# The first batch of an attention and feed-forward kernel worked in two parts of its tokens

## The chip, the cores and the metric

The kernel runs on one core of a Trainium2 chip. The core has five engines that work at the same time: TensorE (PE) multiplies matrices, VectorE (DVE) and ScalarE (ACT) work element by element and can read the accumulators (PSUM), GpSimd (POOL) does the same without access to PSUM, and SyncE (SP) only issues transfers (DMA). The metric is the device time of one execution in microseconds (us), lower is better, given as the median of several runs.

## What is computed

For 8 batches, 8 heads, 576 tokens and a head width of 64, attention with a threshold, then a feed-forward layer with a maximum over three products:

```python
scores = scale * np.matmul(q, k.transpose(0, 1, 3, 2))
thresh = np.max(scores, axis=-1, keepdims=True) - tau
scores = np.where(scores >= thresh, scores, -1000000000.0)
attn = softmax(scores)
x = (attn @ v).transpose(0, 2, 1, 3).reshape(4608, 512)
h = np.maximum(np.maximum(x @ w1, x @ w2), x @ w3)   # 512 -> 768
out = h @ w_out                                       # 768 -> 512
```

## The kernel before

**Units of work.** Four heads of one batch make a quad, so there are 16 quads, two for each batch. The 576 query tokens of a quad's heads are worked in nine chunks of 128 rows, and each chunk in two halves `r` of 576 columns (one head, or two half heads). Chunk `c` below 4 and chunk `c + 5` hold the same token block of 128 for the two pairs of heads; chunk 4 holds the last 64 tokens of both. So the softmax of the whole kernel is 144 chunks, 288 halves.

**One half.** PE makes its scores in one of four PSUM slots (`scores`, L285; letter `S`). DVE takes their maximum and writes a copy `z` (`maximum`, L327; `m`). ACT makes a first exponential or a leaky clamp (`exponents`, L342; `e`), and then either ACT makes the exponential with its sum (`n`) or DVE multiplies by the mask with its sum (`k`) (`numerators`, L352). The digits of `MASKED` (L24) choose the form for each half: 1 and 3 leave the mask to DVE, 2 and 3 let ACT read the scores from PSUM instead of `z` (`direct`, L312), and digit 0 needs one more small DVE instruction for the threshold (`s`). When both halves of a chunk are summed, DVE makes the reciprocals (`r`), POOL writes the normalized `P` in bf16 (`p`, two instructions, L366), and SP issues a DMA that transposes `P` into `ptq` (`t`, L376). There are nine buffers for `z`, six for `P`, two for `ptq`, and four PSUM slots for everything that PE writes.

**Around it.** Loads of q, k and v (`l`); transposes of q and k on PE (`T`) with their copies to `qt` (ACT, `a`) and `kt` (mostly DVE, `c`); a copy of `qt` with its halves swapped (`q`, POOL, for the first quad partly DVE); casts of v (`y`, POOL); loads of the 12 weight pieces of 512 KB (`g`, SP) into two staging buffers and their casts (`z`, POOL). The staging buffers serve as two more `z` buffers after half 72.

**Products and feed-forward.** When a quad's chunks are transposed, PE multiplies them with v (`product`, L381; `O`), and DVE and ACT copy the result to `xt` (`w`, `x`). When both quads of a batch are there, the feed-forward of the batch (`ffn`, L440) makes 18 pieces `hid` (six blocks of 128 hidden columns, three weights each; `F`, and `B` for the second half of a whole piece). The first of three is copied by ACT (`h`, tile `hm`), the other two are folded in by DVE with a maximum (`v`, tiles `hm` and `hT`). Then follow two output pieces of two token blocks each (also `F` and `B`, copied out by ACT, `u`, stored by SP, `o`) and one for the last 64 tokens (`N`, `j`, `i`).

**The split.** `SPLIT` (L38) names batches that are worked in two parts of their tokens: blocks 0 and 1 (256 tokens), then blocks 2, 3 and 4 (320 tokens). For such a batch `steps` (L553) lists the chunks of the first part for both quads, then those of the second part for both quads; `products` (L591) and `ffn` make products and 18 hidden pieces for each part. A piece of a part uses all 128 rows of PE at once and has 4 matmuls of 256 or 320 columns; a piece of a whole batch has 16 matmuls of 64 rows and 288 columns, of which two run side by side. Before the change only batch 7, the last, is split.

**The order.** Everything is issued in the order of the string `ORDER` (L40), one letter for each step as named above; a digit behind `S`, `T`, `O`, `F` or `N` is the PSUM slot. Each engine keeps this order (`_Ordered`, L84), so an engine that waits holds up all that stands behind it on that engine. The loop that reads the string is at the end of the kernel:

```python
while x < len(text):
    what = text[x]
    if what in "STOFN":
        x += 1
    issue(what, int(text[x]) if what in "STOFN" else None)
    x += 1
```

Since every instruction passes through one helper, the profile names line 93 for nearly all of them, and groups are told apart by their tiles.

Of the kernel before, what the change touches and what calls it, by code (L numbers as in the profile page):

```python
# [39 lines left out]
ORDER = """  # L40
llllllllT0T1gacgT2qqlaT1lqqS2clS1lmlS0zmlS3mlS2enemlznmS1lS3ersmlpS2eklS0pelmnlmyS3germeS1plkptS2eemnT0mlmS1
lrS3enskplelermlpnT2smS1tnpS3mapmtT0qascqeT0rS2tpecmepS0nkqtS1nT2rmnqmlepslkeS3ylakeS2rmynplS0epgmeS1tpsmeyT
3rnmS2tnpS1npmnystrS2rmpespemS0eqctT2mqT3enkpS0lnssS1rlaplnS2lqermtpemS0pesS1clpnmlS3npmlertmpnkS1petresT2mn
pS0keqlS3rtempmpkS0tpS1mennasrtremS2pempmS3ytzeseS2mS0pnmS1npmS2nytssmT0erceT1pleO3pmlektO0swernpgS3nlpmalwk
S3nlrS1xmlpnS0mlpeS3tmyT1eS2rssmpnS0spemeymO2zeceygO0wntrkpS3xwrS2nsstS0pmnF1pmnBtpsesF2mF3hqrT0nyBqaF1rsveB
zF0vnT2qgT3clqBaBzhS3evF1qgnmtBpS0evpS3nrF2mlpS1eslmpS0ntmyS3pesmS1pnslmS0ztBrmT3hpF1ceF2pgeBmlzF3esvlBnBgvF
1etkF0hBrkepBtsnvS3S2nprmeS1ptmF3epvBrqmtS0hS2spmeS3zsmS1leF0lsknpF2nBmBeytmS3essvS1qerlkO0pngerslvpnlmO2pnm
pnrswS3peS1wremzF0emBqgnktpS1hS3xmS0nptmS2pF1rsmepBtsnF0vT3sraS1mteBqT2evT3pnmS0ptacS1zemS3eS2pmeS0ztmemqnF3
mlerklpeS2sBlkelpeF1mlklS2klS0leuunrsmS3pnoBkpnlmelO2uqmlnrlkO3ptwrqrT2weexkS0uptF3nmS1BsysclF0phmF2tyeBpseS
1vyBetmS3npF0vnS1prmBnptS2mhyS3rspsmS1eS0ytmepF2mnF3pBmelBvlF0enssS1klF2erlmBpeoBvphF1osnF3vlBeklBntS2svT0hr  # L50
rT1mpnF3tcapS2espS0metT1prmBnyF2srvnT0tByceS3qsvaS0plemF1qlnS2mBnqmS0hpS3srsmeF2ptmS1epS0meBptmS3qS1vF0penns
smF2yteBmBersvS1phT3sskpF0aT2keF3mnBrBqtnvO1pnveprN0rceptS3wnpS2mjS1ptsS0mepS3rmeF2ptmnpmnS0BsetkekS3urlmpS1
ulmeqS0lmT2epS3mlaS1nmlO2nrlmplesO3kqoekleO1klewslswxS0pxlrwT2nmS3plS1nrcplF0ermptempS2S3pmlS1penmBoemqonkF3
tF1ekeBkF2lhBrkutpF3uvBBryssvelS1lhS0ympT2lS3matpS1mnS2pseF0ssmtF3emT1eBsrcpF2teBrvpeBpeS0vtS1npmS3nmS0thmF1
nS2smtnF3kF0esBsrmepBsvBnpS2hvtS1nrF0rmpnT3BmlpaS2vlepS1mtS3eqS0mnpF2semF1lBersmopT3nBstcyF0pevO3erktphkBnsF
1weoS2rpvnlF3qmBelBnvqtT2T0hrqsS1capS3lemF2pnS0mptS1nssmBpeS3mytF0evS1nyBmelO2ssrvepmepN3wxktS1nS2rmpnS0mpS1
esrjmyS2tnpS3meF0psrmleptskeT1pS2eBmelmqalS3kqnS2lmS1ntrmeO3puqmuO2oysnswlerkyT0lS3ewlrcF1pxiskepS0emS2tnpmB
nqmelpkS0ulF2puT3lmeBlF1rrskhplS0akF2teBmBnsvpF0tnS3spveBpmS1lhS2srtmepS0meF3pF1esmtyF2ekBnBvtBnsrS0sphrS3mn
lpS2melpF0mntF3pBveqS2ssveBorS1nsmopF0emtpS2eBrvpS1hsmlF3pnS0monT2mlBnF1rclpeF0vlBpeBtvynT3S2shqS1amtF0eykT3
eO2sscterkO3pnmewqBxT1nwqvS2npF3mS0aytsrBrnpmF1espvS2eS0rpmtS3empBS2mphtF0nsspsT3mBeqcF2tnS1veS3rmT0peBmpaS1  # L60
ssvS3eqtS0semqN2nmqlS1mjlnS3klS0nF2lremppmO1yenrtsmeO3wynpipT0xwBcnlrkeplS3kulS0umS1lnS2mpteS3mF0ermpetF1epm
T2BsslkekalF3uklBuF2strrkhpBesBvnS1lpF0voepS3metS2prBmpS1hmtS3pnmF0ynS2rssmptBnS1mpeF3svqetF2sBmeBkeF1lkF0nB
vhBerrvF3pnS2spvBnmptS1eS0rpmhT2epmlT3S1acplF0eosS3mnBtmF1nvT2eF3ktBBssceS0rvhS2pesrO1mpemytnsS3wnpS2mS1lnpm
F0nqtF3ssmeBqBsrevqF1leS2pvlnS0mplBemS3lhF2srmtepS0S1epmF3nmBtnBsrkpT1nvO0npvT2xtwrrS3spacS0eymS1peS2mptS3em
S0pemF1qetmnsskT2BalkelrmS3nlpS2slumqS0elsmpO3eomuoN2erkplO0ekljwelS1rpeoF3kxqtnwS2mnS0ympS1nlF2pmlBqmoenssi
seBkF1khT0iuBrrscpuS2veF0ptS3mnpS1mepS2oemBoF3mF1treesvBpBrkhpT0lF2katS3vnBmnF0ytT1vnBpcS3hpS2tmeS0reF1smpS3
etsmqF2nBmqeT0kF3paBvnBrnstsS1vpS0hrmpeS2mptF1erS3spmeS0spmnlBF2lmqeF3lqsessvBtyeBpvS1hS0rkpntF3mnF2mBpnlS1r
snvpT0tBecpO3metveS0snrwF2plnS1mpS3ermBytepmS0hT1mS3aT2smnT0qN1capnF3rkqF2teBsssesBvqjS0leS1qveS3pmF2nprmnpm
tS0nS1spmnT3ByretrcempS0usS3pumS1eptmS2eF0pmemnS1kBesskermO2pnknyO1keteskyO3xrwuwpuS2wxptS0empS3erS1mptS2emp
F0mF3lBmBlenkhF2ntvS0nS1ssrmBpelF3vpeF0smBteBsrhkF1peF2vBnyS0nvS3pnmO1ntmS0wrsrS3rpesmS1eymBpS0shptmF3nF2pmn  # L70
BprtBevS0peS1vpF3oemF2pnomBoBrhsskpS1teF3veF0mpBetkBS1vhF2tnrkF0pnBmF3esprBveBytvpO2nkO1pxhS0rwS2mptS1mpS0mS
# [649 lines left out]
```

## Time and profile before

| | |
|---|---|
| median of 3 runs | 455.76 us (454.06 to 458.42) |
| the profiled execution | 457.37 us, of which the span from the first to the last instruction is 455.6 us |
| PE, weight loads of PE | busy 429.6 us (94%), 318.8 us (70%) |
| DVE, ACT, POOL | busy 398.0 (87%), 403.5 (89%), 314.7 us (69%) |
| granted clock of PE | 0.984 of full speed as a mean |
| DMA | 87.46 MB, mean 192 GB/s |

The time of a run holds some 1.8 us beside the span. A line of a stage shows the stretch in us from the span's start, its length, then for each engine the busy time and in brackets the number of instructions, and at the end the granted clock of PE, the mean busy share of the 16 DMA engines and what they moved in GB/s. A line of the chain of waits shows start, length and the work that the end of the kernel hung on. A line of a group shows line, engine, operation, written tile and read tiles, their shapes and the count; then busy time in us and the mean of one in ns; then the idle time of the engine just before, and what ended it.

### The profile page before, as it was taken

The numbers are of one execution on the slowest core, as the hardware profiler recorded it, in microseconds if no ns is written. First come the engines' busy times: TensorE is split into PE (matmuls) and PEld (weight loads), VectorE is DVE, ScalarE is ACT, GpSimd is POOL, SyncE is SP. The second block draws the span as 40 slices with busy tenths as digits, with TensorE's granted clock in tenths as the row PEclk, the third lists the DMA queues.
The fourth block names the chain that finished last, engine by engine and source line by source line (L and its number), as shares of the span: only waits on it lengthen the run. The fifth ranks groups of instructions, "written<-read, shape, count | busy, mean of one in ns | idle before, by whom it ended". The sixth has DMA issues, their size and how long they took to land. (4 is left out here: it accounts for less than half of the span.)

```text
span 455.6 us, 14387 instructions
## 1 busy us (share of the span) xinstructions
PE 429.6 (94%) x5188; PEld 318.8 (70%) x5188; DVE 398.0 (87%) x1256; ACT 403.5 (89%) x830; POOL 314.7 (69%) x416
## 2 busy tenths in 40 slices
...
GB/s 261 237 232 177 239 185 201 221 227 266 187 223 179 217 185 231 195 211 197 166 232 201 206 190 226 159 237 159 158 221 198 225 149 124 116 199 127 128 82 105
DMA packets 213287, 87.46 MB, mean 192 GB/s; under 512 B 186336, under 2 KB 200160, under 8 KB 213216
## 3 DMA queue, kind: packets, MB, share of 16 engines
...
## 5 line engine op out<-in xcount | busy, mean ns | idle before, releaser
L93 POOL TENSOR_SCALAR P<-z,rs 128x576 bf16<-128x576 f32 x250 | 202.0, 820 | 77.9 <-DVE rs L93 31.1
L93 DVE TENSOR_SCALAR_CACHE_REDUCE z<-sc 128x576 f32<-128x576 f32 x250 | 182.1, 751 | 13.2 <-PE sc L93 7.6
L93 PE MATMUL sc<-kt,qs 64*128 64x256 f32 (+2 forms) x640 | 180.0, 425 | 7.7 <-DVE z L93 3.4
L93 PE MATMUL sc<-kt,qt 64*128 64x320 f32 (+2 forms) x640 | 182.3, 436 | 3.8 <-DVE z L93 3.2
L93 PE MATMUL ph<-xt,w 64*128 64x288 bf16 (+2 forms) x2160 | 165.1, 283 | 0.3
L93 PEld LDWEIGHTS <-w 64*128 64x128 bf16 (+1 forms) x2160 | 126.6, 94 | 29.9 <-issue 4.4
L93 ACT ACTIVATE z<-z,th 128x576 f32<-128x576 f32 x154 | 114.3, 768 | 6.6 <-DVE th L93 4.2
L93 ACT ACTIVATE z<-z 128x576 f32<-128x576 f32 x174 | 117.0, 674 | 0.3
L93 PEld LDWEIGHTS sc<-kt,qs 64*128 64x128 f32 (+1 forms) x640 | 93.2, 180 | 29.6 <-DVE z L93 5.5
L93 PEld LDWEIGHTS sc<-kt,qt 64*128 64x128 f32 (+1 forms) x640 | 93.2, 180 | 22.9 <-DVE z L93 12.8
L93 DVE SCALAR_TENSOR_TENSOR z<-z 128x576 f32<-128x576 f32 x76 | 61.3, 817 | 0.6 <-ACT z L93 0.5
L93 PE MATMUL po<-wo,hT 64*128 64x512 bf16 (+1 forms) x480 | 53.9, 356 | 0.2
...
L93 ACT ACTIVATE z<-z,nm 128x576 f32<-128x576 f32 x68 | 50.9, 767 | 0.6 <-DVE z L93 0.6
L93 DVE TENSOR_TENSOR hm<-ph,hm 128x576 bf16<-128x576 f32 (+2 forms) x54 | 37.1, 686 | 12.7 <-PE ph L93 10.8
L93 ACT ACTIVATE hm<-ph 128x576 bf16<-128x576 f32 (+2 forms) x54 | 31.9, 590 | 17.4 <-PE ph L93 16.9
L93 PE MATMUL o<-ptq,vb 128*64 128x64 bf16 (+2 forms) x544 | 40.0, 281 | 2.5 <-DVE z L93 0.9
L93 PEld LDWEIGHTS <-hT 64*128 64x128 bf16 (+1 forms) x480 | 29.4, 97 | 17.1 <-issue 3.0
L93 DVE TENSOR_TENSOR hT<-ph,hm 128x576 bf16<-128x576 f32 (+2 forms) x54 | 37.2, 688 | 4.2 <-PE ph L93 1.6
L93 POOL TENSOR_SCALAR P<-stage,rs 128x576 bf16<-128x576 f32 x38 | 28.9, 766 | 17.1 <-DVE rs L93 8.2
L93 PEld LDWEIGHTS <-vb 128*64 128x64 bf16 x544 | 25.2, 111 | 15.1 <-issue 7.0
L93 ACT ACTIVATION_READ_ACCUMULATOR z<-z 128x1 f32 x174 | 33.5, 192 | 0.0
...
## 6 DMA issues: line engine op xcount, KB each, us to landing
...
ptq<-P SPq DMA_TRANSPOSE x144, 4.2
...
```

Of the source, the lines that this page charges most:

```text
L93: ins = fn(*a, **kw)
```

## The change

Batch 0 is entered in `SPLIT` beside batch 7, and `ORDER` and `MASKED` are made anew for it. No function is changed.

```diff
-SPLIT = {7: ((0, 1), (2, 3, 4))}
+SPLIT = {0: ((0, 1), (2, 3, 4)), 7: ((0, 1), (2, 3, 4))}

 MASKED = """
-223012122203003302220200300102301202300201021000200000000110010010000010
...
+122232002223223221222033020010000001230030020101021210200000010001000001
...
 ORDER = """
-llllllllT0T1gacgT2qqlaT1lqqS2clS1lmlS0zmlS3mlS2enemlznmS1lS3ersmlpS2eklS0pelmnlmyS3germeS1plkptS2eemnT0mlmS1
-lrS3enskplelermlpnT2smS1tnpS3mapmtT0qascqeT0rS2tpecmepS0nkqtS1nT2rmnqmlepslkeS3ylakeS2rmynplS0epgmeS1tpsmeyT
...
-3iS2mF1eeesketF0BsmBmoN3vO2jrO1vpxnkO3pskF0xetnwF2repreBpknptBurupF1uptF0hpF3vF1vtF0hF3vF1vF0ihF3vF1vF0ohF3v
-F1vF0hF3vF1vF0hF3uvN1vO2jiO3wF1xooF3oF2hF0vF3vF2hF0vF3vF2hF0vF3vF2hF0vF3vF2hF0vF3vF2hF0vBvF0uuoBoN1uuojoi
+lllllllglT0lT1alT2cqlaT0qlS2clllllylzlllyqqS0mS1mS2mS3mS0ekenemeS1nrmS2nmlpmT1gpesaskgT2qlT1rclT3aqlectqS1eq
+epS3nynyrmS0nmzS2ermepS1gmnS3lpmntpermzS0etepkS2eS1pnS3mnmptnrmpempgS0ekpteS3meS2rS1ymnlpmntpmzkS1tS0S3eeenr
...
+pO1vmtF2eweF3kF1hF0nrvF3pvnF2vpF1hF0vtrF3vphF2vF0pvF3htF2vvF2ooBooO3O0xO1wxF1F0hF3vF1vF0huF3vF1ovF0hiF3vF1vF
+0hF3vF1vF0hF3vF1vF0huF3vovF3BN0uuojoi
```

Over the whole kernel the new strings have 171 digits 0, 78 digits 1, 28 digits 2 and 11 digits 3, against 177, 82, 21 and 8. There are 36 narrow hidden pieces more and 18 whole ones fewer, eight narrow products more and four whole ones fewer; the output pieces are as many as before.

In the old order the first product stands behind the 18th `r` and the first hidden piece behind the 23rd; in the new one they stand behind the 12th and the 14th. The scores of quad 1 begin after 8 score halves instead of 18.

How many steps of a kind stand in the string up to the 24th, the 54th and the 144th (last) `r`, old order and new:

| step | 24th: old | new | 54th: old | new | 144th: old | new |
|---|---|---|---|---|---|---|
| score halves `S` | 54 | 55 | 115 | 114 | 288 | 288 |
| transposed parts `T` | 16 | 16 | 30 | 28 | 64 | 64 |
| whole hidden pieces | 3 | 0 | 36 | 18 | 126 | 108 |
| hidden pieces of 256 columns | 0 | 18 | 0 | 18 | 0 | 31 |
| hidden pieces of 320 columns | 0 | 0 | 0 | 18 | 0 | 18 |
| output pairs | 0 | 0 | 2 | 3 | 14 | 14 |
| whole products | 4 | 0 | 9 | 6 | 28 | 24 |
| products of 256, of 320 columns | 0, 0 | 4, 2 | 0, 0 | 4, 4 | 4, 2 | 8, 5 |
| ninths `N` | 0 | 0 | 1 | 1 | 6 | 7 |
| `e`: from PSUM, from `z` | 23, 27 | 26, 26 | 26, 84 | 30, 79 | 29, 259 | 39, 249 |
| `n`, `k` | 36, 13 | 37, 13 | 79, 29 | 80, 28 | 198, 90 | 199, 89 |
| `h`: whole, 256, 320 | 1, 0, 0 | 0, 6, 0 | 12, 0, 0 | 6, 6, 6 | 42, 0, 0 | 36, 10, 6 |
| `v`: whole, 256, 320 | 0, 0, 0 | 0, 11, 0 | 24, 0, 0 | 12, 12, 12 | 84, 0, 0 | 72, 19, 12 |
| `s` | 24 | 19 | 62 | 58 | 177 | 171 |
| `p`, `t` | 46, 22 | 46, 21 | 106, 52 | 104, 52 | 285, 142 | 286, 143 |
| weight loads `g`, casts `z` | 6, 4 | 12, 10 | 12, 12 | 12, 12 | 12, 12 | 12, 12 |
| swaps `q`, v casts `y`, other loads `l` | 13, 10, 46 | 16, 7, 43 | 29, 21, 78 | 28, 21, 81 | 64, 48, 162 | 64, 48, 162 |

More of the change, by code (lines that the diff above doesn't have):

```diff
@@ L24 @@
 MASKED = """
-223012122203003302220200300102301202300201021000200000000110010010000010
-001111121020120000101000000001010000001120111020011110000001000010010000
-010010100110010110000100000001100000100000011011110000011000010000000010
-110011000011100001101000010000000100000100111300011000000011100101110010
+122232002223223221222033020010000001230030020101021210200000010001000001
+010102311002001000000010101000100000111110232010000010000010000001000101
+000300110112000001000110000000010100011110020111000100010000110010000000
+010111110100010000010000001010001000000111110011000100000010010113010122
 """
@@ L36 @@
 PBUFS = 6
-SPLIT = {7: ((0, 1), (2, 3, 4))}
+SPLIT = {0: ((0, 1), (2, 3, 4)), 7: ((0, 1), (2, 3, 4))}
 ORDER = """
-llllllllT0T1gacgT2qqlaT1lqqS2clS1lmlS0zmlS3mlS2enemlznmS1lS3ersmlpS2eklS0pelmnlmyS3germeS1plkptS2eemnT0mlmS1
-lrS3enskplelermlpnT2smS1tnpS3mapmtT0qascqeT0rS2tpecmepS0nkqtS1nT2rmnqmlepslkeS3ylakeS2rmynplS0epgmeS1tpsmeyT
-3rnmS2tnpS1npmnystrS2rmpespemS0eqctT2mqT3enkpS0lnssS1rlaplnS2lqermtpemS0pesS1clpnmlS3npmlertmpnkS1petresT2mn
-pS0keqlS3rtempmpkS0tpS1mennasrtremS2pempmS3ytzeseS2mS0pnmS1npmS2nytssmT0erceT1pleO3pmlektO0swernpgS3nlpmalwk
@@ L45 @@
[L45 to L69, printed above, removed]
@@ L70 @@
-F0mF3lBmBlenkhF2ntvS0nS1ssrmBpelF3vpeF0smBteBsrhkF1peF2vBnyS0nvS3pnmO1ntmS0wrsrS3rpesmS1eymBpS0shptmF3nF2pmn
-BprtBevS0peS1vpF3oemF2pnomBoBrhsskpS1teF3veF0mpBetkBS1vhF2tnrkF0pnBmF3esprBveBytvpO2nkO1pxhS0rwS2mptS1mpS0mS
-3iS2mF1eeesketF0BsmBmoN3vO2jrO1vpxnkO3pskF0xetnwF2repreBpknptBurupF1uptF0hpF3vF1vtF0hF3vF1vF0ihF3vF1vF0ohF3v
-F1vF0hF3vF1vF0hF3uvN1vO2jiO3wF1xooF3oF2hF0vF3vF2hF0vF3vF2hF0vF3vF2hF0vF3vF2hF0vF3vF2hF0vBvF0uuoBoN1uuojoi
+lllllllglT0lT1alT2cqlaT0qlS2clllllylzlllyqqS0mS1mS2mS3mS0ekenemeS1nrmS2nmlpmT1gpesaskgT2qlT1rclT3aqlectqS1eq
@@ new lines @@
+epS3nynyrmS0nmzS2ermepS1gmnS3lpmntpermzS0etepkS2eS1pnS3mnmptnrmpempgS0ekpteS3meS2rS1ymnlpmntpmzkS1tS0S3eeenr
+srpmS2lnpmlnymleprgS3epmtnT1pmpeskT3etS0rkpS2lenmlszseS0mapgrT2mS1lapcetO0psmnO3qeS2tqxS1mnzO3mnO2rgeprskS1t
+xpesswnwlqnF3rmtqS0heT1pmS3eF2pcS0svpteF1mF2ynsmS3hlnpvS2rmlepF1nvzmS1epgsS2emerF0mpF1eskpS3nkhemS1nvzF3nF0v
+grmS3ptrvF1pmS0penhssS2etmpO1emzO0nswlkeS2leT1rmtpT3ersT2zcakgeS3ptS1nmnpmF3alprvT1nlF2qxF3rlvS0qchelS2mpS1g
+smS3qelmpF2teepvF0mS2nptvF3mqF0ehkF2ntS3vnrS1spmeS0prtmezmnS1setskO0zeO3wnvlS0pnlF2pmnlyxrlmS1epS3tsskepBnml
@@ new lines @@
+ersS0mptnS1rpmS3npmF0utysurF1syhF2evtS0pmeS1pmeF3lysemF0plhsvF1nvlT2nvT0lrS3kaplT1emF2larpcS3thS1npmS0nqsT2s
+lmF3eqlcF1etpvS2evS3qsermO1qtnkpnO0smlnywtepF2rwmxF1yhrS0tevpS2smnS1peF3smptF0evF2pmhnF3ktF1nvT0rhrT2vpaT1sc
+S3peF0meptF2vnpS3vaS0tkeF2merslmnS1pS3lempBlmleekN3utkS1jrnS0pmluS3qmnS1lqmS2elS0mpelO3ssmleorekpO2tewnkpS1x
+woS3smeF2lqmnF0tqBmnS1ysrhsyS3mpnlBpF2melF1evtF3errT0skpBelcBBslvhpS0elvyS2nF1mtpS3nmF0pnmBonBsssrlvS3phS2lm
+epF0tmeS1S3sermpS2temBpeS1smS3etrvpF2nmF0pnBmtnF1svBnrS3skphlBemF0leT2ryvlByaplS3vnF1lpmS2elpS0sresmtT3yBemF
@@ new lines @@
+2npcS0thyBskpnT3O1kaemO3nrstrpvewpS0xwlqS2nmS3teqmF1F0nymqBeosskF3qeBvT2hBrprceS1psvF2nS0pmteS3mpBnmS1ptnS0v
+pnS3mF2terrmpS1mpS0mptF3eeesempekBlktBkeklS1klS0reuuuurmlpnS2imS3pesT0mpelN1mpalS2kqlS0rejT3tnO1cynsmeopO3mn
+lywpnlT2S0swxsorkS1paiS3emF2rpmnF0tBsepmS1hpT3meBtqF2sceF1qvnBtqrS3nrpvBnS0mptS2hmpS3emT1ytF0yasssrS2meBpsml
+eF3pF1vtnBpeBvS0thsF2mnF1knBoBevlF0rnrS3vplS2eslmpBemS1ptnS3mphS2rsmelpS1S0stempF3nssqmF2nBtsmF1evBeBlvnF3lk
+S0hlS2emBoemT1lT0esrrO2vplascpnO3keptwnT1F0wepcS2xqstF1emS3ynryBmqlS2nvqBlnS3mphlS0mpnS2lsF1rertmpF3emBpeBss
@@ new lines @@
+vptS2nS0pveT1ktF3asknrS1erpmBempemptS0usS2spumS1eqmtS0emqS2F3klmlT1eneklBnrsmpncS0pnS2mutO1urrkpeO3lewplermN
+1plxwkelT2pS3alS0jmnF2pomS1nptS3ssmeBqsrF0emqtF1hskpBeBsvnF2tyT3evBnS0ryclyS1hpmlS3empS2tS0mpF1rmF3plBmtpBvS
+0yennnsS2rsemtF1pemF0pnBvtS2khS3nsmBeF1rmpF2evBpeBvtS0hsrS3skepF2semlF1lepmBlBnsvF3tnsrS0vnT2mBalT1khS0qlceS
+2leO3sympemqnS1wS2pnsrrT3mpF0tamT1npS3cBnplrmS1epoF2ssveS3qtmBepS0mnqF1omnF3ptsBkeF0eBsrvphlBnT2ptvO1eyveokS
+3xS0twarsmpS1nrS2mpnS3lmpF0etmpermS1pelBkptkF3meneusstkS2ukS1eS0rerompBomplempT1ulS2cyuS0lnmT3lpS1amS2tnT3sm
@@ new lines @@
+S0esO1rnmlpnorsqcO2elmqelwpS3xwlS0sepmF2lepmS1leS3qtmF0nqmBnyBsstkhF3kF1eBrevtpS2eBvpF0hskyiF3nBrmyeF1lvBetp
+BkF0pT2ehvBaT1ytvnF3qS2rncqS0nmBpT1mN2asrskF0qjevS1S2epmS3nmptBF1sprhsrmS2eptS0mnS3pmeS2ptmS0pBmF3rensvtepF2
+BsempBevlS0hkF1lnS3smlS2nmiBeO0rsmpntskqeO3vewpS2xktS0nF1srwempS3eBmlpF2nlmF0nrlrBvpT3trhBsspsceS1pvF3ntS2mp
+nBmpeS1vtS0yeyS2smeF3mpnrmtpS1S0pmS2mBtennsrkepS0meoS1umpS2umteT0S3rskpnF1malkeplT2BleclemlT0eskN2luO3kulesk
+oO1jrrlkapetwS2xwpT0nmF1qleS3scS2lpnmBntqS0mS3hprmS2epiF1mF0pesrresBsmtqF3esvBqeS2povBtpS1mhS0pmeS3mnpF2oF1m
@@ new lines @@
+ntBknS3nF0mtBnsrBvpeF3lvpS2eBsshytmF1esF0sveT2rBrkpaBvnT3S2hycS1pnmF0ptnT3mBperS2veqtS1ssmaqS0erF3mpnS2mpBem
+S1ptS0esvpnS2mS3etrmO1pnmqnlO0sskqelswlF2xymT1eBrwcpeS3sS0hptmS1epmS2eF3mtF0nkBnF1srvonpBsBlnpmF3hrtrF2kpeBv
+eT1BvlpaT0eT3tvqS1ascqN2nsqS0jrmeS3pmS2npS1meF0ptsmepmnT3qS2tnrS1pmeBmpectF2ekeS3uiS1nmBnkurkS3pukO0uemO2ssp
+ewterpS1wxmS0pkF2lF3omBoBmhF1lrevF2ptnBpBvS3lehsrF0kpnF1tmF2ekBpBsvBrtF3vphF0pF2BlBvtBsS1vhS3emS2erS0mpS1nmy
+S3eympF2smF0etBmnBssnvF3F1esrvpF2nkBynBrF0hrBevpF3eBptvBhpsS2evytS0ynmpF3nmS1pS2smetBmeO1rO0sspwevS2xpnS1mS3
@@ L74 @@
+tnmS0nS2rmpeO1mpO3ewN0tskxeS1kjS3ermopF0emopnmF1tnkkF3esrF2khpeBrrepS3kuptBuvnmpS0usS3pumtF2erpF1vS0mptF2ehn
+pO1vmtF2eweF3kF1hF0nrvF3pvnF2vpF1hF0vtrF3vphF2vF0pvF3htF2vvF2ooBooO3O0xO1wxF1F0hF3vF1vF0huF3vF1ovF0hiF3vF1vF
+0hF3vF1vF0hF3vF1vF0huF3vovF3BN0uuojoi
 """
```

## The prediction

> **What bounds the kernel now.** I read the clock line and the 40 slices first, then the busy time of each engine stage by stage, then the chain of waits at the end. The stages are cut where DVE runs its 24th, 54th and last (144th) reciprocal, at 75.9, 165.3 and 423.2 us: one reciprocal closes the softmax of one chunk, so the number of reciprocals measures progress alike in both orders.
>
> ```profile
> core 0: us, PE busy (x) PEld busy (x) DVE busy (x) ACT busy (x) POOL busy (x), PEclk, DMA share, GB/s
> 10.00:75.90 65.90, 51.86 (x450) 32.35 (x449) 58.18 (x192) 61.92 (x131) 53.70 (x69) 0.92 1.01 212
> 75.90:165.30 89.40, 87.78 (x1111) 64.78 (x1107) 81.25 (x255) 83.77 (x173) 72.70 (x96) 1.00 1.08 216
> 165.30:423.20 257.90, 256.63 (x3320) 197.62 (x3318) 244.32 (x781) 244.57 (x503) 183.61 (x242) 1.00 0.98 186
> 423.20:455.60 32.40, 27.49 (x268) 19.02 (x262) 11.60 (x26) 10.16 (x23) 2.38 (x4) 0.99 0.40 105
> ```
>
> In the first stage PE stands idle for 14.0 us, because there is no feed-forward work yet; ACT is busy 61.92 of 65.9 us and sets the pace. In the second and third stage PE is busy 98 and 99.5%, ACT 94 and 95%, DVE 91 and 95%: PE leads, but ACT and DVE follow closely. The last stage is the work that only PE can still do:
>
> ```profile
> 424.31 7.96 PE ph L93 x72
> 432.28 0.78 PE po L93 x12
> 433.05 1.41 PE o L93 x40
> 434.46 1.40 PE po L93 x12
> 435.86 9.89 PE ph L93 x72
> 445.75 2.11 PE po L93 x19
> 447.86 2.36 DMA out_dram<-ob
> ```
>
> Here the last P ends at 425.58 on POOL's timeline, and the products that need it begin only at 433.05, after the feed-forward pieces of the last batch's first part.
>
> **Prices.** The split pieces already stand in the trace, in the last batch: 18 narrow pieces take 7.96 us of PE (0.442 each) for 256 columns and 9.89 (0.549) for 320. A whole piece is 16 matmuls; the chain has 0.49 us for 8, so 0.98. So the split costs PE nothing: 0.99 against 0.98. A score half is 0.485 us (0.97 for 8 matmuls in the chain), a whole product 1.36, a narrow one 0.60 or 0.70 (1.21 and 1.41 for two), an output pair 2.6 (1.29 for 12 of its 24 matmuls), a ninth 0.78. The evictions:
>
> ```profile
> L93 DVE TENSOR_TENSOR hT<-ph,hm 128x576 bf16<-128x576 f32 x42 | 31.7, 754 | 2.9 <-PE ph L93 1.6
> ...
> L93 ACT ACTIVATE hm<-ph 128x576 bf16<-128x576 f32 x42 | 26.9, 641 | 5.1 <-PE ph L93 4.7
> ...
> L93 DVE TENSOR_TENSOR hT<-ph,hm 128x320 bf16<-128x320 f32 x6 | 3.0, 492 | 0.6
> ...
> L93 ACT ACTIVATE hm<-ph 128x320 bf16<-128x320 f32 x6 | 2.6, 437 | 7.6 <-PE ph L93 7.6
> L93 DVE TENSOR_TENSOR hT<-ph,hm 128x256 bf16<-128x256 f32 x6 | 2.6, 425 | 0.6
> ...
> L93 ACT ACTIVATE hm<-ph 128x256 bf16<-128x256 f32 x6 | 2.3, 383 | 4.6 <-PE ph L93 4.6
> ```
>
> Two narrow evictions cost more than a whole one: ACT 383 + 437 - 641 = 179 ns, six times; DVE 425 + 492 - 754 = 163 ns, twelve times. Neighbours on an engine overlap at their ends: ACT's groups, count times mean, add up to 476 us where the engine is busy 403.5, DVE's to 482 where it is busy 398.0, so sums of means are scaled by 0.85 and 0.83.
>
> **The change part by part**, by the table of counts at the three marks (new less old).
>
> *To the 24th reciprocal.* ACT: six hm of 256 columns for one of 576 (+1.66), two more first exponentials of which three more read the scores directly (3 x 0.728 - 0.768 = +1.42), one more second exponential (0.674 + 0.192 = +0.87), three narrow xt at the prices of hm for two at 592 ns (+0.02): 3.97, scaled +3.3 us. DVE: eleven narrow maxima (+4.68), other xt copies (-0.60), five thresholds fewer (5 x 0.144 = -0.72): scaled +2.8. PE: 18 narrow pieces, six narrow products and a score half, less three whole pieces and four whole products: +3.9, into 14.0 us of idleness. POOL: six more weight casts at 1.037 us, three more swaps at 0.714, three fewer v casts: +6.4, beside 12.2 us of idleness. SP issues six more weight loads at about 0.5 us and three other loads fewer; it waits for POOL's P for 114.5 us over the run, so they fit in. Their 3.1 MB are 14.8 us of DMA at the 212 GB/s of this stage, nothing at 268 GB/s (the first 10 us), which would leave room for 3.7 MB; I take nothing, since the weights are asked for well before their pieces. ACT paces this stage: the cost is between 0 (its 4 us of idleness take it up) and +3.9 (PE's, if nothing overlaps). I take +2.5, nearer to ACT's.
> Quad 1 is also needed sooner, after 8 score halves instead of 18. Its k was issued at 11.31 and such loads land in 6.0 us (median), so at 17.3; 8 maxima at 0.834 us keep DVE fed from 10.49 to 17.2. Bounds 0 and +2 (transpose, copy and swap behind the load); I take +0.5.
>
> *From there to the 54th.* The difference shrinks: PE from +3.9 to +2.6, so -1.3; ACT from +3.3 to +1.2, -2.1; DVE from +2.8 to -0.1, -2.9. PE is the fuller here, so between -1.3 and -2.9; I take -2.0.
>
> *From there to the 144th.* PE to +5.8, so +3.2: the new order has 13 narrow pieces of the last batch done before the last reciprocal, the old none. ACT +3.2, DVE +2.7. PE has 1.3 us of idleness there, so +1.9 to +3.2; I take +3.2.
>
> *After the last reciprocal.* PE has 5.8 us less to do. But the cover shrinks too: five narrow pieces (2.2), an output pair (2.6) and one product that is ready (0.7) make 5.5 us, while the last P (two of 0.82 behind the reciprocal) and its transpose (3.52 and 4.64 us in the chain) need 6 to 7. PE would wait 0.5 to 1.5 us, and perhaps 0.9 for the copies of xt, since no output pair now stands between the last products and their pieces. So -3.2 to -4.4; I take -3.7.
>
> *Sum*: 2.5 + 0.5 - 2.0 + 3.2 - 3.7 = +0.5. The profiled execution took 457.37 us (span 455.6), so 457.9 of its kind; it lies 1.6 above the median 455.76, so **456.3**. The early work fills PE, but where ACT was the pace, and it comes back as PE time only partly.
>
> **Rivals.** *A, faster: ACT, not PE, is the bound all along.* PE's weight loads fill only 77% of the third stage. If PE is not full, the other engines' waits close once work is spread: at the 97% that ACT reaches in 20 to 70 us, stage two is (83.8 - 2.1)/0.97 = 84.2 us (-5.2) and stage three (244.6 + 3.2)/0.97 = 255.5 (-2.4). With 2.5 + 0.5 - 3.7 that is -8.3: 449.1 of its kind, 447.5 as median. Against it: by the back-to-back prices above that stage holds 173 score halves (83.9), 90 whole pieces (88.2), 12 output pairs (31.2), 25 products (29.6), five ninths (3.9) and 34 transposed parts (about 0.43 each by the chain, 14.6): 251 of 257.9 us. [...]
> *B, slower: the weight casts.* POOL is in order, and each cast waits for its load in front of the P that frees a z buffer. At the 17th reciprocal POOL has 7.8 us more to do (five weight casts, two v casts, two P), DVE only +3.0. It decides from the point where POOL's idle time of that stretch (8.0 us in 10 to 60) is used up; then P comes late, the nine z buffers fill, DVE stops, and stage one costs +7.8 instead of +2.5: +5.8 in all, 461.6 as median. Against it: DVE waited for P only 2.8 us in the whole run.
> *C, the clock in the tail.* In stage one a PE wait of 1.51 us was followed by this:
>
> ```profile
> 30.00:32.00 2.00, 0.99 (x4) 0.33 (x4) 2.00 (x8) 1.74 (x5) 1.90 (x3) 0.86 0.92 172
> 32.00:34.00 2.00, 1.47 (x7) 1.33 (x8) 1.36 (x5) 2.00 (x5) 1.85 (x3) 0.50 0.54 154
> ...
> 36.00:38.00 2.00, 2.00 (x16) 1.31 (x12) 1.19 (x3) 2.00 (x7) 1.69 (x4) 0.50 1.18 319
> ```
>
> Half a clock for some 7 us. If the wait ahead of the last products does the same, their pieces lose 3.5 us: 459.8 as median. [...]
>
> **How the numbers follow.** Forecast 0.45, A 0.23, B 0.22, C 0.10. About 1% (4.6 us) is what a measurement of this kernel can tell from no change: faster means below 451.2, slower above 460.3. A gives most of faster (0.20), the lower edge of the forecast 0.04; B gives 0.18 of slower, C 0.04, stage one at its bound 0.07: 0.24, 0.47, 0.29. The range runs from just under A, 446, to B with the quad 1 wait and half of C's loss, 464. The forecast alone spans 450.4 (all lower bounds) to 460.4 (all upper).
>
> **What would show it.** First ph near the 14th reciprocal instead of the 23rd; PE idle before 76 us down to about 10 us; the 24th reciprocal near 79, the 54th near 166 and the last near 427 us, with the span's end some 29 us behind it. A shows as a 54th reciprocal before 163; B as DVE z waiting for POOL P for over 5 us before 80; C as a clock near 0.5 behind the last products. I am wrong if the marks move the other way, above all if stage three is shorter.

## The result, and the profile after

| | before | after |
|---|---|---|
| median of 20 runs each | 454.77 us (454.06 to 458.42) | 457.48 us (455.07 to 460.64) |
| ratio of after to before | | 1.006, interval 1.0045 to 1.0075 |
| profiled execution, its span | 457.37, 455.6 us | 457.86, 456.1 us |
| PE, its weight loads, DVE, ACT, POOL busy | 429.6, 318.8, 398.0, 403.5, 314.7 us | 430.8, 316.2, 398.7, 404.2, 310.1 us |

The change is a loss of 2.7 us by the medians: small, but outside what the interval allows for no change, and inside the one per cent that the prediction called "within 1%". The two profiled executions stand only 0.5 us apart, because the one of before lies 2.6 us above its median and the one of after 0.4 us above its own.

The helper that names most groups stands in line 94 of the changed kernel. The stages of the changed kernel, cut at its own 24th, 54th and last reciprocal (81.9, 165.5 and 428.1 us; before 75.9, 165.3 and 423.2):

```profile
10.00:82.00 72.00, 58.78 (x498) 36.43 (x496) 61.35 (x195) 65.48 (x140) 59.50 (x76) 0.90 1.03 234
82.00:165.50 83.50, 81.87 (x960) 60.02 (x958) 78.33 (x256) 80.89 (x173) 63.54 (x86) 1.00 1.04 205
165.50:428.10 262.60, 262.20 (x3369) 199.99 (x3366) 246.93 (x785) 248.15 (x510) 183.97 (x245) 1.00 0.95 183
428.10:456.10 28.00, 21.13 (x214) 13.92 (x211) 8.64 (x20) 6.61 (x15) 1.47 (x2) 0.98 0.35 107
```

Against the four lines of before: stage one is 6.1 us longer, stage two 5.9 shorter, stage three 4.7 longer and the tail 4.4 shorter. PE's idleness in stage one is 72.00 - 58.78 = 13.2 us where it was 14.0. The early feed-forward work did not fill it: 9.9 of the 13.2 us lie before the first hidden piece, which starts at 52.1 us (9.7 us in before, up to the same time), where that work cannot reach. Stages two and three are as full of PE work as before.

A single mark misleads here. The order around one reciprocal differs between the two strings, and the mark jumps with it: the 21st comes 2.5 us later than before, the 24th 6.1, the 27th 3.4, the 36th 1.7. So from here on a mark is the mean over the eleven reciprocals about it (at the end, over the last six). By it the changed kernel is 2.8 us late at the 24th, 2.3 at the 44th, 0.8 at the 54th, 1.9 early at the 117th and 4.5 late at the end of the reciprocals.

The chain of waits at the end:

```profile
424.60 5.38 PE ph L94 x48
...
430.07 0.44 DVE hm L94
...
430.60 0.44 DVE hT L94
...
431.08 1.49 PE po L94 x12
...
432.61 1.47 PE po L94 x12
434.08 2.25 PE o L94 x60
...
436.36 0.45 ACT xt L94
...
436.84 9.41 PE ph L94 x68
...
446.35 0.50 DVE hm L94
...
446.94 0.50 DVE hT L94
...
447.49 1.49 PE po L94 x12
```

In before PE stood in this chain without a gap from 424.31 to 447.86. Now three evictions lie bare in it: PE stands from 429.98 to 431.08, from 436.33 to 436.84 and from 446.25 to 447.49, 2.85 us together. The old order kept the second half of an output pair for the place ahead of the last output pair; the new one issues it at once, and nothing is left to put there.

### The profile page after: what moved, and what is told of

The parts are those of the page before. It is cut to its first block, busy times and chain, and to the rows that moved or that the text cites. A ratio compares the mean times of both kernels' runs of the same rounds, so it can differ in the third digit from the quotient of the medians.

```text
span 456.1 us, 14192 instructions
## 1 busy us (share of the span) xinstructions
PE 430.8 (94%) x5084; PEld 316.2 (69%) x5084; DVE 398.7 (87%) x1260; ACT 404.2 (89%) x840; POOL 310.1 (68%) x416
## 4 chain that ended last, share of the span: by engine, by line
PE 75%; ACT 7%; DVE 6%; POOL 4%; issue 3%; DMA 2%; SPq 0%; ACTq 0%; DVEq 0%; POOLq 0%
PE ph L94 29%; PE sc L94 27%; PE po L94 9%; PE o L94 7%; ACT z L94 5%; DVE z L94 5%; PE tp L94 3%; POOL P L94 3%; DMA qm<-in_q_dram 1%; DMA ptq<-P 1%; ACT qt L94 1%; DVE hm L94 1%; ACT stage L94 0%; POOL vb L94 0%; POOL wo L94 0%
## 5 line engine op out<-in xcount | busy, mean ns | idle before, releaser
L94 POOL TENSOR_SCALAR P<-z,rs 128x576 bf16<-128x576 f32 x250 | 199.1, 809 | 92.7 <-DVE rs L94 49.0
L94 PE MATMUL sc<-kt,qt 64*128 64x256 f32 (+2 forms) x640 | 181.6, 439 | 6.7 <-DVE z L94 3.5
L94 PE MATMUL sc<-kt,qs 64*128 64x320 f32 (+2 forms) x640 | 179.7, 426 | 3.8 <-DVE kt L94 1.3
L94 PEld LDWEIGHTS <-w 64*128 64x128 bf16 (+1 forms) x2016 | 123.2, 95 | 36.9 <-issue 13.5
L94 ACT ACTIVATE z<-z 128x576 f32<-128x576 f32 x172 | 115.7, 676 | 0.1
L94 ACT ACTIVATE z<-z,th 128x576 f32<-128x576 f32 x145 | 108.4, 768 | 5.1 <-DVE th L94 4.1
L94 PEld LDWEIGHTS sc<-kt,qs 64*128 64x128 f32 (+1 forms) x640 | 94.8, 181 | 25.6 <-DVE z L94 4.6
L94 PEld LDWEIGHTS sc<-kt,qt 64*128 64x128 f32 (+1 forms) x640 | 94.4, 181 | 22.2 <-DVE z L94 6.9
L94 DVE SCALAR_TENSOR_TENSOR z<-z 128x576 f32<-128x576 f32 x78 | 63.4, 823 | 0.9 <-ACT z L94 0.8
L94 PEld LDWEIGHTS <-hT 64*128 64x128 bf16 (+1 forms) x480 | 28.8, 97 | 19.9 <-issue 4.1
L94 PEld LDWEIGHTS <-vb 128*64 128x64 bf16 x576 | 23.4, 112 | 15.0 <-issue 6.7
```

The costliest lines, as they stand in the source:

```text
L94: ins = fn(*a, **kw)
```

## The experiments

In the table, the first four columns of times are the profiled execution's differences to the profiled execution of before, in us: at the 24th and 44th reciprocal (means over eleven), what is gained or lost from the 44th to the 117th, and from there to the end of the span. The ratio is of many runs to runs of the kernel before beside them. A star marks a stretch with a seam in it, a place where two orders are joined.

| kernel | 24th | 44th | 44th to 117th | 117th to end | ratio, interval |
|---|---|---|---|---|---|
| changed kernel | +2.8 | +2.3 | -4.2 | +2.4 | 1.006 (1.0045 to 1.0075) |
| new until 52nd, then old | +2.7 | +2.1 | +0.7* | 0.0 | 1.008 (1.0049 to 1.0111) |
| new until 44th, then old | +1.6 | +1.5 | +1.1* | 0.0 | 1.0066 (1.0041 to 1.0091) |
| new until 119th, then old | +0.2 | -0.3 | -3.6 | +1.3* | 1.0012 (0.9993 to 1.0031) |
| new until 126th, then old | +1.4 | +0.9 | -3.4 | +3.1* | 1.0052 (1.0029 to 1.0074) |
| old until 57th, then new | -1.1 | -1.1 | +0.8* | +2.6 | 1.0086 (1.0058 to 1.0115) |
| old until 44th, then new | -1.3 | -0.3 | -1.8* | +2.7 | 1.0059 (1.0038 to 1.008) |
| old until 119th, then new | -0.4 | -0.4 | +1.3 | +4.8* | 1.0115 (1.009 to 1.014) |
| PE kept busy | +11.7 | +11.2 | -3.3 | +2.4 | 1.0265 (1.0227 to 1.0304) |
| no early evictions | +0.5 | -0.1 | -2.7 | +2.6 | 1.002 (0.9993 to 1.0046) |
| short early pieces | +3.0 | +1.8 | -1.8 | +2.4 | 1.0073 (1.0044 to 1.0102) |
| doubled evictions | +2.9 | +2.2 | -4.1 | +2.5 | 1.0064 (1.004 to 1.0088) |
| tail filled | +0.9 | +0.3 | -1.4 | +3.2 | 1.0059 (1.0031 to 1.0087) |

### Which part of the order loses: three kernels with one seam

Each follows one of the two orders up to a reciprocal and the other behind it; the masks go with the order. All compute the whole reference.

New start, old rest from the 52nd reciprocal (against the changed kernel):

```diff
-2npcS0thyBskpnT3O1kaemO3nrstrpvewpS0xwlqS2nmS3teqmF1F0nymqBeosskF3qeBvT2hBrprceS1psvF2nS0pmteS3mpBnmS1ptnS0v
...
+2npcS0thyBskpnT3O1kaemO3nrstrpvewpS0xwlqS2nmS3teqmF1F0nymqBeosskF3qeBvT2hBrprcS0mS0T2sspaT1eF2mnBqtnvpnveprc
...
```

> The new order up to its 52nd reciprocal (the split first batch and all that belongs to it), and from there the steps that are left in the old kernel's order. In the changed kernel the 54th reciprocal stands only 0.2 us behind the old one's, with 2.4 us more of PE's work done. Theory (the split start neither loses nor gains, the 0.6% come from the re-made rest): a ratio of 0.998 to 1.001 to the kernel before. Rival (the lead in PE's work is kept to the end): 0.995 or less. Second rival (the loss is made by the start): 1.004 or more.

Old start, new rest from the 57th (against the kernel before):

```diff
-ulmeqS0lmT2epS3mlaS1nmlO2nrlmplesO3kqoekleO1klewslswxS0pxlrwT2nmS3plS1nrcplF0ermptempS2S3pmlS1penmBoemqonkF3
...
+ulmeqS0lmT2epS3mlaS1nmlO2nrlmplesO3kqoekleO1klewslswxS0pxlrF3BuuiN2jtyeopmnypnlS0wsornS2piS3emF1rpmnF0tBsepm
...
```

> The converse: the old kernel, first batch whole, up to its 57th reciprocal, and from there what is left in the new order. Theory (the loss lies in the re-made rest): a ratio of 1.005 to 1.010. Rival (the loss is made by the split start): 0.998 to 1.002.

New until the 126th, old end (against the changed kernel):

```diff
-eT1BvlpaT0eT3tvqS1ascqN2nsqS0jrmeS3pmS2npS1meF0ptsmepmnT3qS2tnrS1pmeBmpectF2ekeS3uiS1nmBnkurkS3pukO0uemO2ssp
...
+eT1BvlpaT0eT3tvqS1ascqN2nsqS0jrmeS3pmS2npS1meF0ptsmepmnT3qS2tnrlnBrcempS1uS3pumS0eptmS2eF1pmemnS0kBesskermpk
...
```

> The new order up to its 126th reciprocal, and from there the old order. The changed kernel stands 1.0 us ahead of the old one at the 126th reciprocal, with 1.9 us more of PE's work done, and 4.9 us behind at the last. Theory (the new order loses its lead in the last 18 chunks, where it does seven hidden pieces and the first products of the last batch sooner): 0.994 to 0.999. Rival (the last stretch only pays for work that the old order does after its last reciprocal): 1.004 to 1.007, as the changed kernel.

Measured: 459.52, 459.86 and 457.9 us. The first two, which take nearly opposite parts of the change, are both slower than the whole change, so they add up to far more than it (0.008 + 0.0086 against 0.006): the seam itself costs. By the ratios, the first lies with its second rival (the start loses), the second with its theory (the rest loses), and the third with its rival; the theory that the split start costs nothing was missed. In the first, the nine reciprocals from the 45th to the 54th took 26.0 us, against 21.6 in before and 22.2 in the changed kernel; in the second, those from the 54th to the 63rd took 32.2 against 26.2 and 28.8. So these three cannot be added up, and the next four were cut where the two orders had the most work in common at the seam.

### Four kernels cut where the orders match

New until the 119th reciprocal, then old; new until the 44th, then old (both against the changed kernel):

```diff
-ntBknS3nF0mtBnsrBvpeF3lvpS2eBsshytmF1esF0sveT2rBrkpaBvnT3S2hycS1pnmF0ptnT3mBperS2veqtS1ssmaqS0erF3mpnS2mpBem
...
+ntBknS3nF0mtBnsrBvpeF3lvpS2eBsshytmF1esF0sveT2rBrkpaBvnT3S2hycS1pnmF0ptnT3mBperS2veqtS1ssmaqS0erF3mpnS2mpoeS
...
```

> New order up to its 119th reciprocal, then the old order, cut where the two orders have the same steps behind them but for two whole pieces, one ninth and two casts; so the seam should cost little, unlike the cuts at the 52nd and 57th, whose stretch of nine chunks at the seam took 26 and 32 us where the kernels take 22 and 26 to 29. At the 119th reciprocal the changed kernel is 1.7 us ahead of the old. Theory (the early part ends a little ahead, and the loss is made in the last 25 chunks): ratio 0.993 to 0.998. Rival (the lead at that mark is only a matter of which step DVE does first): 1.000 to 1.004.

```diff
-epF0tmeS1S3sermpS2temBpeS1smS3etrvpF2nmF0pnBmtnF1svBnrS3skphlBemF0leT2ryvlByaplS3vnF1lpmS2elpS0sresmtT3yBemF
...
+epF0tmeS1S3sermpS2temBpeyynnF1snF3vlBenlBkvT0hrrT1mpnF3tcapS2espS0metT1prmBkyF2srvnT0tByceS3qsvaS0plemF1qlnS
...
```

> New order up to its 44th reciprocal (batch 0 in two parts, its feed-forward, and a third of batch 1), then the old order; at the cut the orders differ by one score half, one ninth and a few casts. This is the split with the old rest. At the mark the changed kernel is 1.5 us behind. Theory (the split by itself neither gains nor loses): 0.999 to 1.004. Rival (the start makes the loss of 0.6%): 1.005 or more.

Old until the 44th, then new; old until the 119th, then new (both against the kernel before):

```diff
-1vyBetmS3npF0vnS1prmBnptS2mhyS3rspsmS1eS0ytmepF2mnF3pBmelBvlF0enssS1klF2erlmBpeoBvphF1osnF3vlBeklBntS2svT0hr
...
+1vyBetmS3npF0vnS1prmBnptS2mhyS3rspsmS1eS0ytmepF2mnF3pBmelBvlF0enssS1klF2erlmBpeoBvphN3joS1tS0smS3etrvpF1mF2p
...
```

> The converse: old order, first batch whole, up to the 44th reciprocal, then the new order. Theory (the loss lies in the re-made rest, above all its end): 1.003 to 1.007. Rival (the start makes the loss): 0.998 to 1.001.

```diff
-etsmqF2nBmqeT0kF3paBvnBrnstsS1vpS0hrmpeS2mptF1erS3spmeS0spmnlBF2lmqeF3lqsessvBtyeBpvS1hS0rkpntF3mnF2mBpnlS1r
...
+etsmqF2nBmqeT0kF3paBvnBrnstsS1vpS0hrmpeS2mptF1erS3spmN2jiyyBvF1BemS3ptS0esvpnS2mS1etrmO3pnmqklO0ssnqselswlF2
...
```

> Old order up to the 119th reciprocal, then the new order. Theory (the loss lies in the last 25 chunks): 1.007 to 1.011. Rival (it does not): 0.998 to 1.002.

Measured: 455.79, 459.01, 458.2 and 461.07 us. The first two ratios lie with the rivals, the third with its theory, and the fourth just above its theory's range: taken by themselves, start and end both lose. Each pair of complements sums to nearly the same: 0.0012 + 0.0115 = 0.0127 and 0.0066 + 0.0059 = 0.0125, where the whole change is 0.006. If a seam costs the same everywhere, it costs half the excess, 0.0033 or 1.5 us, and the parts are: up to the 44th reciprocal +1.5 us, from there to the 119th -2.5, from there to the end +3.7. That the seams are equal is an assumption; by the table they are not quite. At the late cuts the stretch with the seam costs 1.3 and 3.1 us with the old end, and 4.8 - 2.5 = 2.3 with the new one.

The table says much the same by another way, without that assumption. Eight executions run the new end without a seam in it. Seven of them lose 2.4 to 2.7 us there, whatever came before (the eighth, with a mended tail, 3.2), and with the old end the loss is 0.0 twice. That the end is a loss is the firmest finding of the study. The middle of the new order gains 1.4 to 4.2 us in eight executions without a seam in it, against 0 and a loss of 1.3 with the old one. The new start stands at -0.3 to +2.3 at the 44th in six unaltered executions, a mean of +1.1, against 0, -1.1 and -0.4 with the old start: about +1.6. The signs are surer than the sizes: start, middle and end so read add up to about +1 us, the medians to +2.7, for the column rests on single executions, and the one of before lies 2.6 us above its median.

### Does the slow clock pay for the start?

From about 42 to 49 us of the changed kernel PE's clock is half; the first products, which stand ahead of score halves, begin in that stretch, at 45.1 us. Columns as in the stages; the last fence is DVE's own timeline there, with start, length and the wait ahead of the instruction:

```profile
40.00:42.00 2.00, 1.27 (x8) 0.30 (x4) 2.00 (x9) 1.51 (x4) 1.29 (x2) 0.98 0.86 175
42.00:44.00 2.00, 1.99 (x16) 1.47 (x20) 1.34 (x6) 1.45 (x3) 2.00 (x3) 0.50 1.31 224
44.00:46.00 2.00, 2.00 (x18) 0.91 (x16) 1.87 (x6) 2.00 (x5) 1.90 (x4) 0.50 1.11 230
46.00:48.00 2.00, 2.00 (x22) 1.15 (x18) 0.06 (x2) 1.04 (x3) 1.61 (x2) 0.50 0.49 65
48.00:50.00 2.00, 2.00 (x24) 0.95 (x18) 1.11 (x3) 1.84 (x5) 0.00 (x0) 0.81 1.08 313
```

```profile
48.89 0.76 DVE L94 TENSOR_SCALAR_CACHE_REDUCE z<-sc 128x576 f32<-128x576 f32 x1 [2.83 <-PE sc L94]
```

PE works through two products at half speed, and DVE, with 0.06 us of work between 46 and 48, waits 2.83 us for the next scores. It is the longest wait for scores in this stage. The experiment puts two matmuls of 128 columns behind each of 28 early score halves, in columns of the accumulator that nobody reads, so that PE does not pause:

```diff
+    number_of_s = iter(range(1 << 20))
...
+        if 8 <= next(number_of_s) < 36:
+            for _ in range(2):
+                tensor.matmul(ps[:, 0:128], identf, identf, start=True, stop=True)
```

> The changed kernel with two extra matmuls behind each of the score halves 8 to 35, into columns of their PSUM slot that nobody reads. They fill PE's idle time in the first stage, so that its clock is not lowered. Theory (the first stage lost 3 us more than forecast because PE ran at half clock where the early products stand ahead of scores, and DVE starved): the clock stays near 1.0 from 15 to 60 us, the 24th reciprocal moves from 81.9 to 78 to 80 us, ratio 0.998 to 1.003. Rival (the evictions of the early pieces on ACT and DVE are the cost, whatever the clock): 24th reciprocal at 81.5 or later, ratio 1.005 to 1.010.

Measured: 467.4 us. The clock did what it should (0.99 in the stage, against 0.90), but DVE's wait for scores rose from 4.9 to 13.0 us. The stage with the extra matmuls, then the row of waits there (us in total, times, longest), then the same row of the changed kernel:

```profile
10.00:91.00 81.00, 73.70 (x613) 46.27 (x612) 61.76 (x198) 66.44 (x140) 59.29 (x76) 0.99 0.89 205
```

```profile
DVE z L94 <- PE sc L94: 13.0, 23, 1.8
```

```profile
DVE z L94 <- PE sc L94: 4.9, 9, 2.8
```

The extra matmuls were busy for 19.9 us and the 24th reciprocal came 8.9 us later than in the changed kernel: both expectations of the time were missed. The trace shows why. The end of one score half, the extra matmuls behind it, and DVE's maximum of that half:

```profile
60.72 0.43 PE L94 MATMUL sc<-kt,qs 64*128 64x320 f32 x1
61.08 0.71 PE L94 MATMUL sc<-identf 128*128 128x128 f32 x4
61.92 0.76 DVE L94 TENSOR_SCALAR_CACHE_REDUCE z<-sc 128x576 f32<-128x576 f32 x1 [0.84 <-PE sc L94]
```

DVE does not start when its scores are there, at 61.15, but 0.13 us after the extra matmuls, which write to the same slot. It is so for 24 of the 28 halves: the maximum starts 0.76 to 0.81 us behind its own scores, where DVE's waits for scores after 20 us end 0.13 to 0.20 us behind them in the changed kernel. So the experiment held back the very scores that it was to hasten, by some 0.63 us each (an estimate, 15 us in all). It does not show that PE's 13 us of idleness are of no use, nor what a full clock by itself would give.

Other runs say more. In the five other executions of the new start the clock from 45 to 47 us was 0.86 to 1.00, and DVE's waits for scores from 43 to 53 us came to 0.2 to 2.1 us instead of 2.8. Over the 20 runs of the changed kernel the time falls by 2.0 us for each 0.01 that the mean granted clock is higher (from 0.976 to 0.994; correlation -0.56); over 49 runs of the five other kernels with the new start by 0.6 us, a weak tie; over 76 runs of the kernel before, taken beside the experiments, not at all (0.06). The mean clocks of the changed kernel and of before are 0.986 and 0.990. So the slow clock seems to cost time in the new order and not in the old, by that slope some 0.8 us of the 2.7; this is an estimate from a correlation, and no run set the clock alone.

### Who pays for the early feed-forward pieces: ACT and DVE, or PE?

No early evictions: the first part of batch 0 leaves out the 18 evictions of its hidden pieces, and POOL clears that half of `hT`, so that the output of those tokens is zero.

```diff
+                if (b, part) == (0, (0, 1)):
+                    return
...
+    pool.memset(h_of(0)[:, :, 0:256], 0.0)
```

> The changed kernel, whose first part of batch 0 leaves out the 18 evictions of its hidden pieces (6 copies on ACT, 12 maxima on DVE); POOL sets that half of hT to zero ahead of stage one. The output of those tokens is therefore zero. Theory of the prediction (ACT and DVE pay for the early evictions, 18 times 0.44 to 0.5 us, some 8 us in all on the two engines that release the scores): the mean of eleven neighbouring reciprocals about the 24th falls back by 2 to 3 us from the changed kernel's, and the time to 454.5 to 456 (ratio to the kernel before near 1.000). Rival (the start is paid in PE's order: products and pieces stand in the one queue ahead of score halves that ACT and DVE wait for): the 24th falls by less than 1 us, the time stays at 457 to 458 (ratio 1.004 to 1.007).

Measured: 456.61 us, ratio 1.002, and a 24th reciprocal at +0.5 instead of +2.8: between the two expectations by the time, and on the theory's side by the mark. But the mark alone proves little, since the unaltered start gave +0.2 to +2.8.

Short early pieces: the same 18 pieces with one matmul of four; three quarters of their sum over the inputs is left out.

```diff
-                    for kc in range(4):
+                    kcs = 1 if (b, part) == (0, (0, 1)) else 4
+                    for kc in range(kcs):
...
-                        tensor.matmul(o, w(slice(0, 128)), m(slice(0, 128)), start=(kc == 0), stop=(kc == 3))
+                        tensor.matmul(o, w(slice(0, 128)), m(slice(0, 128)), start=(kc == 0), stop=(kc == kcs - 1))
```

> The changed kernel, whose first part of batch 0 makes its 18 hidden pieces with one of their four matmuls each (54 matmuls of 256 columns left out, some 6 us of PE's time between about 57 and 90 us); the evictions stay. That part's output is therefore wrong by the three contraction slices left out. Theory that the queue of PE is what the start pays for: the smoothed 24th reciprocal falls by 1.5 to 3 us and the 54th by 4 to 6 (PE is full in stage two), time 452 to 454. Rival (ACT and DVE pay, by the evictions): the 24th stays within 1 us of the changed kernel's 81.9 by the mean over its neighbours, the 54th still falls by 3 to 5, since PE is full there, and the time to 453 to 455. Of the two the mark at the 24th decides, not the time.

Measured: 459.08 us. Six microseconds of PE work less, and no time gained, neither at the 24th (+3.0) nor at the 44th (+1.8) nor over all. The fall at the 54th that both expected (4 to 6 and 3 to 5 us) did not come (+0.2, where the changed kernel has +0.8). The stage shows where some of it went:

```profile
10.00:82.00 72.00, 55.95 (x445) 33.22 (x443) 62.46 (x196) 64.98 (x140) 58.54 (x76) 0.85 1.04 236
```

PE has 53 matmuls fewer than the changed kernel's 498 in the same stretch, but is busy only 2.8 us less, at a clock of 0.85 instead of 0.90: from 62 to 70 us, among the short pieces, the clock is 0.57 where the changed kernel has 1.00. The many runs agree: the clock is 0.980 as a mean of this kernel's 10 runs, 0.986 of the changed kernel's 20. So part of the time saved went into a slower clock, and this run is no clean test of what the pieces' time on PE costs.

Doubled evictions, the counterpart of the first: each of the 18 is done twice over, with PE's work unchanged.

```diff
+                for _ in range(2 if (b, part) == (0, (0, 1)) else 1):
-                if wi == 0:
-                    scalar.activation(out=hm, in_=pv, func=AF.Copy)
...
+                    if wi == 0:
+                        scalar.activation(out=hm, in_=pv, func=AF.Copy)
...
```

> The changed kernel, whose first part of batch 0 makes each of its 18 evictions twice over (the same values written again): 6 more copies of 0.38 us on ACT (2.3 us) and 12 more maxima of 0.42 us on DVE (5.0 us), PE's work unchanged. Theory that ACT and DVE bound the start: the mirror of the run without these evictions, which gave about 1.8 us back; the mean about the 24th reciprocal rises by 1 to 3 us over the changed kernel's, the time to 459 to 460.5, ratio to the kernel before 1.009 to 1.013. Rival (these evictions lie in slack, and the run without them gained by the spread between runs): the mark stays within the 0.2 to 2.8 us that the same start showed, the ratio at 1.005 to 1.007.

Measured: 458.36 us, ratio 1.0064. The groups show that the work was done, 36 instructions where there were 18:

```profile
L94 DVE TENSOR_TENSOR hm<-ph,hm 128x256 bf16<-128x256 f32 x12 | 5.1, 424 | 0.9 <-PE ph L94 0.5
L94 DVE TENSOR_TENSOR hT<-ph,hm 128x256 bf16<-128x256 f32 x12 | 5.0, 420 | 0.3
L94 ACT ACTIVATE hm<-ph 128x256 bf16<-128x256 f32 x12 | 4.6, 381 | 2.7 <-PE ph L94 2.5
```

Half of these lines is extra, 2.3 us on ACT and 5.0 on DVE, and the marks (+2.9, +2.2) and the ratio are the changed kernel's. The rival held: the time of these evictions lies in slack. So the time of ACT and DVE for these evictions is not what the start pays with. That leaving them out gave about 1.8 us back (ratio 1.002 against 1.006, intervals that just meet) while doubling them cost nothing is not explained; a PSUM slot that comes free without waiting for ACT and DVE is a possible reason, which no run here separates.

### Can the tail be mended?

Only the end of the order is changed. The product of quad 14 that is ready (`O3`) goes ahead of the output pair, the pair's first half (`F2`) ahead of the products of quad 15, and its second half (`B`) ahead of the last output pair.

```diff
-pO1vmtF2eweF3kF1hF0nrvF3pvnF2vpF1hF0vtrF3vphF2vF0pvF3htF2vvF2ooBooO3O0xO1wxF1F0hF3vF1vF0huF3vF1ovF0hiF3vF1vF
-0hF3vF1vF0hF3vF1vF0huF3vovF3BN0uuojoi
+pO1vmtF2eweF3kF1hF0nrvF3pvnF2vpF1hF0vtrF3vphF2vF0pvF3htF2vvO3F2ooooO0xO1wxF1F0hF3vF1vF0hF3vF1vF0hiF3vF1vF0hF
+3vF1vF0hF3vF1vF0hF3vBvF3uuoBoN0uuojoi
```

> The changed kernel with only its last few lines of order mended: the product that is ready is put ahead of the first output pair of the last batch, that pair's first half between the products and the hidden pieces that wait for xt, and its second half between the last hidden piece and the last output pair, as the old order has it. Theory that the three bare chains at the end (PE waits of 1.4, 0.7 and 0.5 us for hT and xt behind the last reciprocal) are part of the loss: the time behind the last reciprocal falls from 28.0 to between 26 and 27, the whole time by 1 to 2 us, ratio to the kernel before 1.002 to 1.004. Rival (the tail is bound elsewhere, by the last stores or by the last transposes): the waits move to other places of the tail and the ratio stays at 1.005 to 1.007.

Measured: 457.87 us, ratio 1.0059, and 457.8 - 429.1 = 28.7 us behind the last reciprocal, where 28.0 stood. PE's waits behind 420 us in this kernel, then in the changed one (us in total, times, longest):

```profile
PE o L94 <- DMA ptq<-P: 1.8, 1, 1.8
PE ph L94 <- ACT xt L94: 0.5, 1, 0.5
```

```profile
PE po L94 <- DVE hT L94: 1.4, 2, 0.7
PE ph L94 <- ACT xt L94: 0.5, 1, 0.5
```

The waits for `hT` are gone, and a wait for the last transpose is there instead. The chain of the mended kernel shows why:

```profile
429.15 0.08 DVE rs L94
...
429.47 0.74 POOL P L94
430.21 0.73 POOLq L717
...
430.96 4.91 DMA ptq<-P
...
435.91 1.61 PE o L94 x36
...
438.03 9.94 PE ph L94 x72
```

From the last reciprocal to the first product that needs it, 6.8 us pass, in which the chain stands on POOL and on the transposing DMA, not on PE. The ready work in hand is one product and one output pair. Spent early, it covers that stretch and leaves the evictions bare; kept for the evictions, it leaves the stretch bare. The rival held: the waits moved.

## Why the prediction was right, and where it was not

**The sum.** It said +0.5 us for a profiled execution, 457.9 us; that execution took 457.86. As a median it said 456.3, and 457.48 was measured. The step of the sum that failed is the last one, where the profiled execution of before was put 1.6 us above its median. By 20 runs it is 2.6 above, and the profiled execution of the changed kernel only 0.4 above its own. One execution's time was taken as the kernel's kind; the change in the medians is +2.7, five times the forecast's +0.5. That the two profiled executions differ by just the 0.5 us of the forecast is luck. Where in the profile of before those 2.6 us are was found only in part. Three other executions with the old start are 0.4 to 1.3 us earlier at the 24th, at clocks of 0.95 to 0.98 from 10 to 82 us where this one has 0.92, and one that follows the old order to the 119th is 0.9 later than it at the 117th.

**Stage one, +3.0** to the 24th: +2.8 in the pair of profiles, and about +2.3 between the means of six executions with the new start (+1.6) and four with the old (-0.7). The size was right. ACT's extra work came as forecast (busy 65.48 us, +3.6, for +3.3), but its idleness in the stage, which was to take up some of it, rose from 4.0 to 6.5 us, so ACT did not set the pace alone. And the reason, ACT's extra work, is not borne out for its eviction part: 2.3 us more of such work on ACT and 5.0 on DVE moved no mark. The other part, the exponentials of scores read directly, was not tried. The first hidden piece came forward as foretold, to 52.1 us (the 14th reciprocal is at 50.4) from 74.1, but PE's idleness, which was to fall to about 10 us, is 13.2, most of it ahead of the first piece. The +0.5 within the term that stands for quad 1's loads was not separated by any run.

The raw marks, which the prediction had put near 79, 166 and 427 us with the end 29 behind, are 81.9, 165.5 and 428.1 with 28.0. **To the 54th, -2.0**: from +2.8 to +0.8, -2.0. **To the last, +3.2**: +4.5 - 0.8 = +3.7 (by the last reciprocal alone, 4.9 us late, +4.1, with which the four terms add up to the +0.5 of the spans). **Behind it, -3.7**: -4.4 (by the terms named there the bounds were -3.4 and -5.3, not -3.2 and -4.4). Each within 0.9. But the cut kernels divide the run more usefully than these marks: a gain of about 3 us from the 44th to the 117th and a loss of 2.5 from there to the end. The prediction had booked the end as work that only moves across the last reciprocal, at -0.5 with the whole of stage three. Measured from the 119th reciprocal to the end, in before and after:

```profile
353.70:455.60 101.90, 96.99 (x1179) 72.76 (x1175) 76.86 (x233) 74.51 (x156) 50.96 (x68) 1.00 0.72 139
```

```profile
352.00:456.10 104.10, 97.23 (x1158) 70.63 (x1155) 76.20 (x232) 73.76 (x155) 51.26 (x67) 0.99 0.66 134
```

PE has the same work, 97.0 and 97.2 us, and idles 6.9 us instead of 4.9. Of the waits in the tail the prediction had named two, 0.5 to 1.5 us for the last transposes and 0.9 for `xt`; the second came, as 0.5. In place of the first stood waits for `hT` (1.4 by the table of waits), which it had not named: a size met by another wait. The wait for the transposes was hidden under them, as the mended tail showed with its 1.8 us.

**Rival A, faster,** did not come: the 54th reciprocal stood at 165.5, not before 163, and PE filled 262.20 of 262.60 us of stage three, with its weight loads at 76% of it. The room that the rival read from their share did not show: the stage took 262.6 us, not 255.5.

**Rival B, the weight casts,** is refuted: DVE waited for POOL's P 1.2 us before 82, not over 5, and POOL's idle time ahead of its P in the whole run rose, from 77.9 to 92.7 us where P is made from `z` and from 95.0 to 101.4 us with the P made from the staging buffers.

```profile
DVE z L94 <- POOL P L94: 1.2, 3, 0.7
```

**Rival C, the clock in the tail,** did not come: the granted clock was 0.98 over the tail, 1.00 from 430 to 440 us; but PE did not wait ahead of the last products there. In the mended tail it did, for 1.84 us, and the clock was 1.00 in the 10 us behind. The fall came in stage one instead, where it had stood already.

**What stays open:** why the new start costs some 1.6 to 2.3 us. Where it arises can be read from the traces. Counted by DVE's maxima, one for each score half in both orders, the six executions of the new start are as a mean 0.5 us ahead of the four of the old one at the 31st (45 us), and 2.7 us behind at the 40th (56 and 59 us), where the first products (44 to 46 us) and the first hidden pieces (49 to 52 us) enter. It is not the time of the evictions there, and the run with short pieces does not point to the pieces' time on PE. The order in which PE serves products, pieces and score halves, the exponentials that read scores directly, the earlier second quad and the slow clock are left, and none was isolated. Open too is why the middle of the new order gains.
